# A fused convolution and two feed-forward layers: an accumulator's copy ahead of a rounding, three tiles in other places

## The chip, the core and the metric

The kernel runs on one core of one Trainium2 chip. Its engines are named as the profile names them: PE (TensorE, with PEld for its weight loads), DVE (VectorE), ACT (ScalarE), POOL (GpSimd) and SP, which here issues the DMAs and passes on notes between matmuls. The metric is the device time of one launch in microseconds (us), as the median of several runs. Lower is better.

## What is computed

```python
# x: (2, 4096, 192), weight_gen: (2, 4096, 8, 7), all float32
w = softmax(weight_gen, axis=-1)                   # 7 taps for each of 8 heads
out = sum over k of w[..., k] * x_padded[s + k]    # causal, 24 channels a head
x = out.reshape(8192, 192)
h = x @ w_in                                       # 192 -> 2048
x = where(h > 0, h, exp(min(h, 0)) - 1) @ w_out    # 2048 -> 192
h = x @ w_in2
return (h * clip(h + 3, 0, 6) / 6) @ w_out2        # 8192 x 192
```

## The kernel before

**Tiles and cells.** The 8192 tokens are cut into NB = 16 blocks of 512. Each of the two layers is worked block by block, and in a block the 2048 hidden columns are worked in NQ = 8 steps of 256. One such step is a cell (m, i, q): layer, block, step. There are 256 cells in one sequence, and the loop over n issues the work of cell n and of those around it. What orders the engines is the order in which this loop writes the instructions, for each engine is a queue worked from its head.

**One cell.** `matmuls` writes on PE the first product of cell n (into a pair of PSUM banks, `hset[n % 2]`) interleaved with the second product of cell n - 3 (LAG = 3), which adds into two accumulators: `acca` (two banks, used by alternate blocks) and `accb` (one bank, used by all blocks). Operands are split into a rounded high part and a low part, so a product is made of three. The two halves of the rows of PE are worked at once. After that, for k = 1 and then k = 0, `act_a` (ACT, L459 and L460 in the first layer, L462 in the second) and `gate` (DVE, L476 or L479) make the activation from bank k. `round_g` (ACT, L466) rounds the activations of cell n - 1 to `gh`, and `rest_g` (DVE, L470) makes the low part `gl`. In cells from n = 8 on, these two stand between k = 1 and k = 0, in cells before that behind k = 0.

**End of a block.** Three cells after the last cell of a block, `fold_b` (ACT, L332) copies `accb` to SBUF; one cell later `fold_a` copies `acca` and joins the two. As all blocks share `accb`, the first second-product matmul of the next block waits for the copy at L332.

**Weights.** The weights come as 64-bit floats and are turned into a high and a low part on the chip. A unit is 384 columns of this, of kind "i" (for `w_in`, to `wi`) or "o" (for `w_out`, to `wo`). Its steps: `begin` (ACT, L141: magnitude of the high word, to a work bank in PSUM, `aux` for "i" and `acca[1]` for "o"), s0, s1, s2 (DVE, L145, L148, L152: the float `f`), s3 (DVE, L157: a mask of the exponent, to the SBUF tile `tr`; and ACT, L159: the high part), s4 (DVE, L165: the rest `rr` from the low word `raw` and the mask). In the first layer PE then adds these up in the unit's bank (p5, L170 to L172) and ACT writes the low part out (p6, L177). In the second layer DVE does so (s5 and s6, L181 and L187). From group 4 on, the work bank of the first layer is the SBUF tile `f` itself, and the PSUM bank is used for the sum alone. `tr` and `rr` have two buffers each.

**Order of the weight work.** First-layer units form groups 0 to 8 (one unit, then pairs, then one unit). Groups 0 and 1 are written out ahead of the loop, groups 2 and 3 in cell 0; p5 and p6 of group n + 1 are written in cell n. So p5 of group 2 stands behind all of group 3 that uses the same banks. Second-layer units are steps of a `Stream`: each has a cell at which it begins and one at which it is due (`wtasks`), and the stream spreads its steps over the cells between.

**The convolution.** `attention` does the softmax on DVE and ACT and the products for a block on POOL (for block 0, on POOL and DVE). Block 1 has its products while the first weights are made. `prepare` transposes a block's result on PE into PSUM (L307, L310), ACT makes `xh` (L317), DVE makes `xl` (L319). Blocks 0 and 1 go through `hset[0]`, all later ones through `(acca[i % 2], aux)`. Block 1 is prepared in cell 5, behind p5 of group 6.

Of the kernel before, what the change touches and what calls it, by code (L numbers as in the profile page):

```python
# [9 lines left out]
F32R = mybir.dt.float32r  # L10
U32 = mybir.dt.uint32
# [6 lines left out]
def kernel(  # L18
# [21 lines left out]
    B, S, D = x.shape  # L40
# [4 lines left out]
    P = 128  # L45
# [3 lines left out]
    NF = DFF // P  # L49
    NQ = NF // 2  # L50
    HALO = K - 1
    LAG = 3
    TM = 4
    NB = TP // TM
# [26 lines left out]
    WI = [{k: cpool.tile([P, NQ * UN], F32R, name=f"wi{m}_{k}") for k in "hl"} for m in range(2)]  # L81

    WO = {0: cpool.tile([P, NF, 2 * D], F32R, name="wo0")}
    w_in = [w.bitcast(U32) for w in (w_in1, w_in2)]
    w_out = [w.bitcast(U32) for w in (w_out1, w_out2)]

# [23 lines left out]
    class Unit:  # L110
# [42 lines left out]
                self.f, self.hw, 0xC0000000, self.b, op0=ALU.bitwise_and, op1=ALU.bitwise_or)  # L153

        def s3(self):
            self.r = stage.tile([P, UN], U32, tag="tr", name="tr", bufs=2)
            nc.vector.tensor_scalar(self.r, self.f, 0xFF800000, None, op0=ALU.bitwise_and)  # L157
            hi, _, v = self.parts()
            nc.scalar.copy(hi, v(self.f.bitcast(F32)))  # L159

        def s4(self):
            f = o = self.r.bitcast(F32)
            if self.m == 0:
                o = self.rr = stage.tile([P, UN], F32R, tag="rr", name="rr", bufs=2)
            nc.vector.scalar_tensor_tensor(o, self.lw, 2.0**-52, f, op0=ALU.mult, op1=ALU.mult)  # L165

        def p5(self):
# [130 lines left out]
    def prepare(m, i):  # L298
        X = xts[m, i] = {
            k: act.tile([P, 2, XN], F32R, tag=f"x{k}", name=f"x{k}") for k in "hl"}  # L300
        v = lambda t: t[:, 0].rearrange("p (h c) -> p h c", h=2)
        if m == 0:

            (y, yd), ps = ya.pop(i), hset[0] if i < 2 else (acca[i % 2], aux)
            for t in range(TM):
                for h, p in enumerate(half):
                    nc.tensor.transpose(ps[h][:, t * HP:(t + 1) * HP], y[p, t, 0:P], ident[p, p])  # L307
            for s in range(2):
                for h, p in enumerate(half):
                    nc.tensor.transpose(ps[h][:, HN + s * HP:HN + (s + 1) * HP], yd[p, s], ident[p, p])  # L310
            parts = [(ps[h][:, 0:XN // 2], (lambda h: lambda t: v(t)[:, h])(h)) for h in range(2)]
        else:
            parts = [(zin.pop(i)[:, 0:XN], lambda t: t[:, 0])]

        def split():
            for src, w in parts:
                nc.scalar.copy(w(X["h"]), src)  # L317
            for src, w in parts:
                nc.vector.tensor_tensor(w(X["l"]), src, w(X["h"]).bitcast(F32), op=ALU.subtract)  # L319
            for k in "hl":  # L320
                for a in range(2):
                    later(1 if (m, i) == (0, 1) else 2, X[k][half[1 - a], 1].bitcast(F32), X[k][half[a], 0].bitcast(F32))
        return split
# [213 lines left out]
    for n in range(2 * NQ):  # L537
        c = NQ * (n + 2) if n < NB - 2 else start2 + (NQ if n % 2 else 0)
        groups.append([("io"[n % 2], 1, n // 2)])
        wtasks.append([c - 3, c + (3 if n < NB - 2 else 2 if n % 2 else 6), 1])  # L540
    made, fts = {}, {}

    def want(n):
# [28 lines left out]
    with tc.manual_schedule():  # L572
# [22 lines left out]
        for n in range(len(cells) + LAG + 3):  # L595
# [14 lines left out]
            for k in (1, 0):  # L610
# [3 lines left out]
                if not k and n < NQ:  # L614
                    for u in made[n + 1]:
                        u.p6()
                if k == (n >= NQ) and 1 <= n <= len(cells):
                    round_g(n - 1)
                    rest_g(n - 1)
                if not k:  # L620
                    continue
                for b in order:
                    if n == last[b] + LAG:
                        fold_b(*b)
                for b in order:
                    if n == last[b] + LAG + 1:
                        fold_a(*b)
# [49 lines left out]
```

## Time and profile before

| What | us |
|---|---|
| Median of 3 runs | 1254.43 (1254.25 to 1255.15) |
| The profiled execution, its own time | 1254.88 |
| Its span, first to last instruction | 1253.1 |
| PE busy (matmuls) | 1200.7 (96%) |
| DVE busy | 938.6 (75%) |
| ACT busy | 852.9 (68%) |
| POOL busy | 414.4 (33%) |

Busy is the time in which at least one instruction of the engine ran. PE is never far from full after the first tenth of the span, so a row that names PE as the one that waits is the first thing to look for. The number in square brackets at the end of a row of the timeline is the idle time ahead of it, with what ended it. Two matmuls run at once on the halves of PE's rows, and the recorded end of one is modelled; how much PE lost at a place is read better from the distance between the starts of matmuls than from the bracket. PEclk is the granted clock of PE as a share of 2.4 GHz; 0.50 is 1.2 GHz.

### The profile page before, as it was taken

To read this page: it belongs to the slowest core of one execution; us is meant where nothing else is said; L and a number is where in the kernel's file an instruction comes from. 1 tells how busy PE (TensorE), PEld (TensorE's weight loads), DVE (VectorE), ACT (ScalarE), POOL (GpSimd) and SP (SyncE) were. 2 spreads that over 40 slices of the span, in tenths; PEclk is the share of its full clock that TensorE was granted. 3 is DMA by queue.
4 is the path that set the end of the run, shared out by engine and by line. 5 is a ranking of instruction groups with operands and counts; after the bars stand their busy time and mean duration, and the time that the engine had idled before them with its cause. 6 is when DMAs were issued, how large, how long until landed. Compare 5 with 4: busy or idle time off the path is not lost.

```text
span 1253.1 us, 25450 instructions
## 1 busy us (share of the span) xinstructions
PE 1200.7 (96%) x10176; PEld 1093.3 (87%) x10176; DVE 938.6 (75%) x1224; ACT 852.9 (68%) x1340; POOL 414.4 (33%) x234
## 2 busy tenths in 40 slices
PE   3779999999999999999999999999999999999998
PEld 2457888888898888888888889999999999899996
DVE  7887989888988988898767666666666666666663
ACT  2557877887887887887886565566656655666563
POOL 7435886666787666688000000000000000000000
PEclk9789999999999999999999999999999999999999
DMA  6420222212222211221111111111111111110110
GB/s 158 125 97 27 87 86 87 71 44 60 87 87 87 83 59 35 84 87 51 50 53 44 34 52 51 39 52 52 28 38 52 51 51 39 52 51 25 41 39 26
DMA packets 33686, 75.82 MB, mean 61 GB/s; under 512 B 4644, under 2 KB 17058, under 8 KB 33568
## 3 DMA queue, kind: packets, MB, share of 16 engines
q1 hardware_dynamic: 33568, 74.19, 20.3%
q8 instruction: 80, 1.31, 0.5%
q14 instruction: 38, 0.31, 0.1%
HBM read 36.43 MB, written 12.58 MB: 39 GB/s over the span
## 4 chain that ended last, share of the span: by engine, by line
PE 68%; ACT 15%; DVE 12%; issue 3%; DMA 1%; SPq 0%; DVEq 0%; ACTq 0%
PE h L439 31%; PE acca L439 21%; PE accb L439 14%; DVE gl L470 5%; ACT gh L466 4%; ACT r L459 4%; ACT r L460 4%; DVE r L476 2%; DMA xl<-xl 1%; DVE tr L157 1%; DVE wt L230 1%; DVE aux L148 1%; DMA xt<-in_x_dram 1%; ACT fold L332 1%; ACT aux L141 0%
## 5 line engine op out<-in xcount | busy, mean ns | idle before, releaser
L439 PE MATMUL h<-xh,wi_l 64*128 64x512 f32 x1536 | 566.4, 397 | 1.6 <-ACT wi_l L177 1.6
L439 PE MATMUL h<-xh,wi_h 64*128 64x512 f32 x1536 | 559.0, 397 | 7.6 <-DVE xl L319 7.6
L439 PE MATMUL acca<-gh,wo 64*128 64x512 f32 x2048 | 561.3, 393 | 0.3
L439 PE MATMUL h<-xl,wi_h 64*128 64x512 f32 x1536 | 556.6, 396 | 0.8 <-DMA xl<-xl 0.8
L470 DVE TENSOR_TENSOR gl<-r,gh 128x1024 fp32r<-128x1024 f32 x256 | 377.3, 1474 | 56.7 <-ACT gh L466 55.3
L439 PEld LDWEIGHTS acca<-gh,wo 64*128 64x128 f32 x2048 | 378.4, 185 | 18.5 <-SPq L443 2.4
L439 PE MATMUL accb<-gh,wo 64*128 64x512 f32 x1024 | 326.0, 398 | 9.5 <-ACT fold L332 6.9
L462 ACT ACTIVATE r<-h,three 128x512 f32<-128x512 f32 x256 | 176.2, 688 | 227.3 <-PE h L439 221.7
L439 PE MATMUL accb<-gl,wo 64*128 64x512 f32 x1024 | 321.6, 393 | 0.0
L439 PE MATMUL acca<-gl,wo 64*128 64x512 f32 x1024 | 320.0, 392 | 0.0
L479 DVE SCALAR_TENSOR_TENSOR r<-r,h 128x512 f32<-128x512 f32 x256 | 176.0, 688 | 171.3 <-ACT r L462 170.5
L439 PEld LDWEIGHTS h<-xh,wi_h 64*128 64x128 f32 x1536 | 278.4, 186 | 21.2 <-DVE xl L319 8.1
L439 PEld LDWEIGHTS h<-xh,wi_l 64*128 64x128 f32 x1536 | 279.0, 186 | 15.3 <-ACT wi_l L177 2.9
L439 PEld LDWEIGHTS h<-xl,wi_h 64*128 64x128 f32 x1536 | 278.6, 186 | 13.7 <-DMA xl<-xl 1.5
L466 ACT CAST gh<-r 128x1024 fp32r<-128x1024 f32 x256 | 265.8, 1038 | 1.4 <-DVE r L479 0.8
L476 DVE SCALAR_TENSOR_TENSOR r<-r,h 128x512 f32<-128x512 f32 x256 | 174.1, 682 | 52.0 <-ACT r L460 51.5
L439 PEld LDWEIGHTS accb<-gh,wo 64*128 64x128 f32 x1024 | 185.9, 186 | 24.9 <-ACT fold L332 14.2
L439 PEld LDWEIGHTS acca<-gl,wo 64*128 64x128 f32 x1024 | 189.1, 185 | 8.0
L439 PEld LDWEIGHTS accb<-gl,wo 64*128 64x128 f32 x1024 | 189.3, 185 | 7.9
L265 POOL TENSOR_TENSOR tmp<-xt,wt 128x768 f32<-128x768 f32 (+1 forms) x96 | 193.5, 2016 | 7.0 <-DMA xt<-in_x_dram 0.8
L459 ACT ACTIVATE r<-h 128x512 f32<-128x512 f32 x256 | 152.7, 596 | 61.9 <-PE acca L439 31.3
L460 ACT ACTIVATE r<-r 128x512 f32<-128x512 f32 x256 | 162.0, 633 | 8.1
(102 smaller groups left out, 747.1 us busy)
## 6 DMA issues: line engine op xcount, KB each, us to landing
xt<-in_x_dram SPq DMA_DIRECT2D x14, 960.0 KB, 5.5
xh<-xh SPq DMA_DIRECT2D x64, 192.0 KB, 2.7
xl<-xl SPq DMA_DIRECT2D x64, 192.0 KB, 2.9
raw<-in_moe_w_out_dram SPq DMA_DIRECT2D x16, 384.0 KB, 3.2
z<-z SPq DMA_DIRECT2D x16, 384.0 KB, 2.3
zin<-z SPq DMA_DIRECT2D x16, 384.0 KB, 3.1
out_dram<-ot SPq DMA_DIRECT2D x16, 384.0 KB, 2.3
raw<-in_moe_w_in_dram SPq DMA_DIRECT2D x16, 192.0 KB, 3.3
```

The source lines that it names most:

```text
L148: nc.vector.tensor_scalar(self.b, self.b, 3, 0x3FFFFFF8, op0=ALU.logical_shift_left, op1=ALU.bitwise_and)
L157: nc.vector.tensor_scalar(self.r, self.f, 0xFF800000, None, op0=ALU.bitwise_and)
L230: v.tensor_tensor(w3, w3, mx.to_broadcast(shp), op=ALU.subtract)
L265: eng.tensor_tensor(o.rearrange("p t (h g) -> p t h g", g=G), xk, wk.rearrange("p (t h) g -> p t h g", h=H), op=ALU.mult)
L439: mm = nc.tensor.matmul(o, w, r, start=st, stop=sp).ins
L459: nc.scalar.activation(r, h, AF.Relu, scale=-1.0)
L460: nc.scalar.activation(r, r, AF.Exp, scale=-1.0)
L462: nc.scalar.activation(r, h, AF.Relu, bias=three)
L466: nc.scalar.copy(gg[n][0], rs[n])
L470: nc.vector.tensor_tensor(gl, rs.pop(n), gh.bitcast(F32), op=ALU.subtract)
L476: nc.vector.scalar_tensor_tensor(r, r, -1.0, h, op0=ALU.add, op1=ALU.max)
L479: nc.vector.scalar_tensor_tensor(r, r, 6.0, h, op0=ALU.min, op1=ALU.mult)
```

## The change

Five edits:

- `fold_b` is written ahead of `round_g` and `rest_g` in the cell in which both stand.
- The mask of s3 goes into the unit's PSUM work bank (`self.b`) instead of `tr`, for units of groups 0 to 3.
- `rr` of the first layer goes into `boot`, a tile with eight places that takes the room of the second layer's `wo1` before that is used, instead of two buffers of its own.
- Block 1 is transposed into `acca[1]` and `aux`, as later blocks are, instead of `hset[0]`.
- In `wtasks` of the last two second-layer units, the "i" unit is due three cells earlier (cell 131 instead of 134), the "o" unit begins and is due two cells earlier (131 to 136 instead of 133 to 138).

```diff
+    boot = cpool.tile([P, NF * 2 * D], F32R, tag="wo1", name="boot")
...
         def s3(self):
-            self.r = stage.tile([P, UN], U32, tag="tr", name="tr", bufs=2)
+            if self.m == 0 and self.n < 4:
+                self.r = self.b
+            else:
+                self.r = stage.tile([P, UN], U32, tag="tr", name="tr", bufs=2)
             nc.vector.tensor_scalar(self.r, self.f, 0xFF800000, None, op0=ALU.bitwise_and)
...
             if self.m == 0:
-                o = self.rr = stage.tile([P, UN], F32R, tag="rr", name="rr", bufs=2)
+                c = (2 * self.n + self.u) % NQ * UN
+                o = self.rr = boot[:, c:c + UN]
             nc.vector.scalar_tensor_tensor(o, self.lw, 2.0**-52, f, op0=ALU.mult, op1=ALU.mult)
...
-            (y, yd), ps = ya.pop(i), hset[0] if i < 2 else (acca[i % 2], aux)
+            (y, yd), ps = ya.pop(i), hset[0] if i == 0 else (acca[i % 2], aux)
...
-        wtasks.append([c - 3, c + (3 if n < NB - 2 else 2 if n % 2 else 6), 1])
+        wtasks.append([c - 3 - 2 * (n == NB - 1), c + (3 if n < NB - 1 else 0), 1])
...
+                if k:
+                    for b in order:
+                        if n == last[b] + LAG:
+                            fold_b(*b)
                 if k == (n >= NQ) and 1 <= n <= len(cells):
                     round_g(n - 1)
                     rest_g(n - 1)
                 if not k:
                     continue
-                for b in order:
-                    if n == last[b] + LAG:
-                        fold_b(*b)
```

How the instructions stand at three places follows. Lines further down than 83 have other numbers in the changed kernel: L141 is L143 there, L152 is L154, L157 is L162, L165 is L171, L187 is L193, L317 is L323, L319 is L325, L332 is L338, L459 and L460 are L465 and L466, L466 is L472, L470 is L476, L479 is L485.

ACT in the cell of the first block end, before; `fold` is the copy of `accb`, `gh` the rounding, and the numbers behind `h` tell the four banks apart:

```order
L459 ACTIVATE r<-h_73 128x512
L460 ACTIVATE r<-r 128x512
L466 CAST gh<-r 128x1024
L332 COPY fold<-accb 128x512
L459 ACTIVATE r<-h_72 128x512
L460 ACTIVATE r<-r 128x512
```

and in the changed kernel:

```order
L465 ACTIVATE r<-h_73 128x512
L466 ACTIVATE r<-r 128x512
L338 COPY fold<-accb 128x512
L472 CAST gh<-r 128x1024
L465 ACTIVATE r<-h_72 128x512
L466 ACTIVATE r<-r 128x512
```

The copy has changed places with the rounding of the cell before; nothing else moved there, and the same holds at the later block ends.

DVE from the second step of group 2 to the first of group 3, with the semaphores that each waits for, before:

```order
L152 SCALAR_TENSOR_TENSOR f<-raw,aux 128x384 [waits DMAHW6_49,DMAHW5_49,DMAHW7_49,DMAHW0_49,DVE_49]
L152 SCALAR_TENSOR_TENSOR f<-raw,acca_77 128x384 [waits DMAHW1_49,DVE_49]
L157 TENSOR_SCALAR tr<-f 128x384 [waits DVE_49] x2
L165 SCALAR_TENSOR_TENSOR rr<-raw,tr 128x384 [waits DVE_49]
L165 SCALAR_TENSOR_TENSOR rr<-raw,tr 128x384 [waits DVE_49,PE_49]
L145 TENSOR_SCALAR aux<-aux 128x384 [waits Activation_49]
```

and in the changed kernel:

```order
L154 SCALAR_TENSOR_TENSOR f<-raw,aux 128x384 [waits DMAHW6_49,DMAHW5_49,DMAHW7_49,DMAHW0_49,DVE_49]
L154 SCALAR_TENSOR_TENSOR f<-raw,acca_77 128x384 [waits DMAHW1_49,DVE_49]
L162 TENSOR_SCALAR aux<-f 128x384 [waits DVE_49]
L162 TENSOR_SCALAR acca_77<-f 128x384 [waits DVE_49]
L171 SCALAR_TENSOR_TENSOR boot<-raw,aux 128x384 [waits DVE_49]
L171 SCALAR_TENSOR_TENSOR boot<-raw,acca_77 128x384 [waits DVE_49]
L147 TENSOR_SCALAR aux<-aux 128x384 [waits Activation_49]
```

The order is the same; the masks lie in the two work banks, and the wait of s4 for PE is gone. In return ACT's L143 of group 3, which writes those banks, waits for DVE in the changed kernel, where L141 before waited for its DMAs alone.

DVE from the `xl` of second-layer block 1 on (cell 132), before; `wi_l` and `wo` are the low parts of the last two units:

```order
L319 TENSOR_TENSOR xl<-zin,xh 128x768
L187 TENSOR_TENSOR wi_l<-aux,tr 128x384
L479 SCALAR_TENSOR_TENSOR r<-r,h_75 128x512
L470 TENSOR_TENSOR gl<-r,gh 128x1024
L479 SCALAR_TENSOR_TENSOR r<-r,h_74 128x512
L145 TENSOR_SCALAR aux<-aux 128x384
```

and in the changed kernel:

```order
L325 TENSOR_TENSOR xl<-zin,xh 128x768
L150 TENSOR_SCALAR aux<-aux 128x384
L154 SCALAR_TENSOR_TENSOR aux<-raw,aux 128x384
L485 SCALAR_TENSOR_TENSOR r<-r,h_75 128x512
L476 TENSOR_TENSOR gl<-r,gh 128x1024
L485 SCALAR_TENSOR_TENSOR r<-r,h_74 128x512
L162 TENSOR_SCALAR tr<-aux 128x384
```

In cell 132 the last "i" unit was being finished, and is now done; the last "o" unit is at its second and third step, where it had not begun. Its low part is written in cell 135, before in cell 137; its first use is in cell 138.

## Rows read from the trace of the kernel before

**Rows 1.** Waits: engine, line, who is waited for: us, times, longest.

```profile
PE aux L170 <- DVE f L152: 21.4, 2, 12.8
...
PEld accb L439 <- ACT fold L332: 14.2, 17, 1.0
...
PE h L439 <- DVE xl L319: 7.6, 2, 5.0
...
PE accb L439 <- ACT fold L332: 6.9, 12, 0.6
...
PE accb L439 <- issue: 2.1, 1, 2.1
```

**Rows 2.** Timeline, ACT at a block's end: start us, us, instruction [idle].

```profile
153.48 1.03 ACT L466 CAST gh<-r 128x1024 fp32r<-128x1024 f32 x1
154.41 0.58 ACT L332 COPY fold<-accb 128x512 f32<-128x512 f32 x1
```

**Rows 3.** Timeline, PE at the same block's end.

```profile
152.21 0.40 PE L439 MATMUL accb<-gl,wo 64*128 64x512 f32 x1
...
153.85 0.40 PE L439 MATMUL acca<-gl,wo 64*128 64x512 f32 x1
...
154.09 0.40 PE L439 MATMUL acca<-gl,wo 64*128 64x512 f32 x1
155.04 0.50 PE L439 MATMUL accb<-gh,wo 64*128 64x512 f32 x1 [0.56 <-ACT fold L332]
...
155.39 0.39 PE L439 MATMUL accb<-gh,wo 64*128 64x512 f32 x1
```

**Rows 4.** Timeline, PE and DVE around PE's stop in the second layer.

```profile
703.60 0.39 PE L439 MATMUL h<-xh,wi_l 64*128 64x512 f32 x1
...
705.35 0.61 DVE L187 TENSOR_TENSOR wo<-aux,tr 128x256 fp32r<-128x256 f32 x2
...
706.07 0.47 PE L439 MATMUL accb<-gh,wo 64*128 64x512 f32 x1 [2.08 <-issue]
```

**Rows 5.** Timeline, DVE in groups 0, 2 and 3, and POOL's last product of block 1.

```profile
12.99 0.79 DVE L157 TENSOR_SCALAR tr<-f 128x384 uint32<-128x384 uint32 x1
...
36.04 0.57 DVE L145 TENSOR_SCALAR aux<-aux 128x384 f32<-128x384 f32 x1 [1.15 <-ACT aux L141]
...
38.83 1.97 DVE L157 TENSOR_SCALAR tr<-f 128x384 uint32<-128x384 uint32 x2
40.72 3.97 DVE L165 SCALAR_TENSOR_TENSOR rr<-raw,tr 128x384 fp32r<-128x384 uint32 x2
...
45.77 0.72 POOL L286 TENSOR_TENSOR y<-y,tmp 128x256 f32<-128x256 f32 x1
...
47.40 0.61 DVE L157 TENSOR_SCALAR tr<-f 128x384 uint32<-128x384 uint32 x2
```

**Rows 6.** Timeline, PE at the end of its first long stop.

```profile
47.07 1.65 PE L170 MATMUL aux<-f,ident 128*128 128x384 f32 x2 [8.63 <-DVE f L152]
```

**Rows 7.** Timeline, PE and ACT around the preparation of block 1.

```profile
83.24 0.47 PE L307 MATMUL h<-ident,y 64*128 64x64 f32 x8
...
84.90 0.54 ACT L177 CAST wo<-acca 128x256 fp32r<-128x256 f32 x2
...
89.11 0.79 PE L439 MATMUL h<-xh,wi_h 64*128 64x512 f32 x1 [5.00 <-DVE xl L319]
...
97.12 0.48 ACT L177 CAST wi_l<-aux 128x384 fp32r<-128x384 f32 x1 [0.16 <-PE aux L172]
...
98.58 0.40 PE L439 MATMUL h<-xh,wi_l 64*128 64x512 f32 x1
```

**Rows 8.** Windows: us, busy of PE, PEld, DVE, ACT, POOL, then PEclk, DMA.

```profile
84.12:86.87 2.75, 0.00 (x0) 0.00 (x0) 1.52 (x3) 2.75 (x7) 2.75 (x2) 1.00 0.17 46
89.11:93.69 4.58, 4.58 (x22) 3.64 (x24) 4.51 (x3) 0.00 (x0) 4.34 (x4) 0.50 0.00 0
703.99:706.07 2.08, 0.00 (x1) 0.04 (x2) 1.41 (x4) 0.69 (x1) 0.00 (x0) 1.00 0.00 0
```

## The prediction

> **What bounds the kernel now.** I read the table of waits first. PE is busy for 96% of the span, so nearly every microsecond PE waits is one that the kernel lasts longer, and what other engines wait for costs nothing by itself. The waits of PE have four large entries [rows 1]: the sum of the first weights waits for DVE's `f` (21.4 us in two waits, of which 12.8 is the start of the program, which the change does not touch, and 8.6 a stop in the start-up), the first product waits for DVE's `xl` (two waits, the longest 5.0), `accb` waits for ACT's copy (12 waits, 6.9), and one wait of 2.1 us has no releaser ("issue"). Then I read the timeline at each of the four. The five edits answer to these four places, and they are far apart in time, so I cost each alone and add.
>
> **The end of a block (first edit).** PE issues a pair of matmuls every 0.24 us (153.85 to 154.09). At the block end the next one comes at 155.04, and the one after it 0.35 later [rows 3]. So the stop costs 0.95 - 0.24 = 0.71, and the slow second pair another 0.11: 0.82, more than the bracket's 0.56. The last matmul into `accb` was over at 152.61 [rows 3], but ACT took the rounding first (153.48) and the copy after it (154.41 to 154.99) [rows 2]. In the changed order the copy starts where the rounding did, 153.48, as its data have been there for 0.87 us, and ends at 154.06. The matmul was due at 154.33, its weights some tenths before, so the stop goes but for a few hundredths. Twelve of them give 12 x 0.82 = 9.8 us. PEld has five more waits for the copy [rows 1]: with about 0.95 for each of the twelve, 14.2 - 11.4 = 2.8 us remain for the five, which PE feels at most in part, as four of them leave no idle time of PE in the table; I take 0.8. **Gain 10.6**, bounds 5 (half of it comes back because ACT runs later than here) and 12.6.
> The rounding and `rest_g` behind it start 0.58 us later (the copy's length). Behind them on ACT stand the activations of k = 0, whose start does not move, since the two ahead of them have only changed places; on DVE the gate of k = 0 stands behind `rest_g`. PE needs this `gh` two cells on. A cell lasts 1253/256 = 4.9 us, so a delay of 0.58 is covered many times over; without that cover it would cost 0.58 at each of 31 block ends, 18 us.
>
> **The last weights (fifth edit).** PE stands from 703.60 to 706.07, and goes on just behind the end of DVE's last `wo` piece (705.35 + 0.61 = 705.96) [rows 4]: the wait called "issue" is one for these weights. The changed table writes that piece two cells, about 9 us, earlier. The step distance less one pair is 2.47 - 0.24 = 2.2, with a slow pair 0.1 more. **Gain 2.3**, bounds 0 and 2.4. The added DVE and ACT steps in the cells before are the same steps, moved to cells where PE does not stand; DVE is busy for 75%.
>
> **The first weights (second and third edit).** The stop is 8.63 us, ended at 47.07 [rows 6]. PE waits there to use the two banks, and DVE must be through the steps of group 3 that use them. Group 2 starts on DVE at 36.04; its first six operations end at 38.83, so one every 0.465, each 0.57 long [rows 5]. These read or write PSUM. The masks then take 1.97 and s4 3.97 for two each, while POOL works on block 1; with POOL done (45.77 + 0.72) two masks of group 3 take 0.61 [rows 5]. What has all its operands in SBUF is held up while POOL runs; what has one in PSUM is not. In the changed kernel s3 and s4 each have one in PSUM, so I take 0.465 apart.
> Now the path in the changed kernel. ACT's next magnitude waits for s4 of the first unit, the new wait: nine operations from 36.04 on end at 36.04 + 8 x 0.465 + 0.57 = 40.33. ACT's operation (taken as long as DVE's on the same 384 columns, 0.57, with 0.1 for the hand-overs) gives 41.0. PE's banks are now free only after s4 of group 3, again nine operations: 41.0 + 3.72 + 0.57 = 45.3. The first unit's mask and s4 save 0.2 each (0.79 against 0.57 [rows 5]), and the whole start with them, 0.4. So PE goes on at 44.9 instead of 47.07. From there to the preparation of block 1 the cells hang on one another through ACT's L177 and the next unit's `f`, so I let the whole stretch move by that. The eight places of `boot` take two waits of DVE for PE away, but DVE waits for ACT's rounding behind them, so I give nothing for that. **Gain 2.2**, bounds -2.8 (below) and 4.
>
> A rule of the Trainium skill speaks against the masks' move: page "VectorE: DVE Perf Modes", section "The perf-mode tier table", gives fp32 `tensor_scalar` two results a cycle with both sides in SBUF, and one when any operand is in PSUM. The trace agrees where POOL is still (0.61 for two, [rows 5]). By that rule alone, an estimate from that page's clock of 0.96 GHz, each of the five masks on this path would be 0.2 us longer, and the sum 1 us smaller instead of larger. The 1.97 and 3.97 for two show that here the other rule weighs more, of page "SBUF — State Buffer", section "Who interferes with whom": DVE in a two-port mode, or with two SBUF inputs, shares ports with GpSimd.
>
> **Block 1 (fourth edit).** PE transposes at 83.24, then waits to 89.11 for DVE to have read `hset[0]` [rows 7]. The granted clock is full for the first 2.75 us of the stop and half from its end to 93.69 [rows 8], which costs another 4.58/2 = 2.3. In the changed kernel the transposes need `acca[1]` and `aux`, which ACT's L177 of group 6 reads until 84.90 + 0.54 = 85.44, a new wait of PE of 2.2 us. With 0.5 for the transposes, PE takes up matmuls at 86.0 instead of 89.11, and a stop of 2.08 us elsewhere did not lower the clock [rows 8], so it should stay up. At full clock the way from there to the low-part matmul of cell 7 (98.58 [rows 7]) is (98.58 - 89.11) - 2.3 = 7.2, so PE would be there at 93.2. But that matmul needs ACT's L177 of 97.12, and this one stands on ACT behind the next unit's high part, made from an `f` that DVE makes while POOL works; nothing of that is freed by the change, and POOL, which waits for these transposes, starts 2.2 us later. If L177 stays at 97.12 + 0.48, PE goes on at 97.65: a gain of 0.9 with a new stop of some 4.4 us. This is near the stop of 5.0, after which the clock was low for 4.58 us of work; that would take 2.3 back. Between +0.9 and -1.4 I take **-0.3**; the upper bound is 98.58 - 93.2 = 5.4, if L177 comes earlier with everything else.
>
> **Sum.** 10.6 + 2.3 + 2.2 - 0.3 = 14.8 us. The profiled execution took 1254.88 (span 1253.1 and 1.8 around it): 1240.1 after the change. The median of the runs shown is 0.45 lower, so I predict 1239.6.
>
> **Rivals.** (1) *The hold-up does not go with PSUM.* If s3 and s4 in PSUM form still take 1.97 and 3.97 beside POOL, group 2 ends at 44.7 as before, ACT's new wait adds 0.7, and group 3 needs 2.8 for six operations and 1.7 for masks and s4 without POOL: 49.9, so 2.8 lost instead of 2.2 gained: 1244.6. Against: the operations with one PSUM operand in the same seconds take 0.57.
> (2) *Block 1 is not held by ACT's L177.* PE then gains 5.4 instead of -0.3: 1233.9. For it: POOL starts later and may leave DVE free for longer.
> (3) *The copy comes no earlier where it counts.* If it then waits for PE's last `accb` matmul, 10.6 is lost: 1250.2. Against: that matmul was over 0.87 us before ACT came.
> (4) *The change does not do what it says for the last weights*: they are written earlier but come late all the same, as their data are not loaded. 1241.9.
> (5) *Slower than before.* The rounding, now behind the copy, comes too late for the second product: 0.58 at each of 31 block ends is 18.0 us, 1257.6. It decides once `gh` and `gl` have less than 0.58 us to spare before PE wants them; the spare is more than one cell, 4.9 us, so this is remote.
>
> **How the numbers follow.** Forecast 1239.6: 0.68. Rival 1: 0.10; rival 2: 0.09; rival 3: 0.06; rival 4: 0.05; rival 5: 0.02. The forecast's own terms spread by about 4 us to each side (block ends 9.5 to 12, start-up 0.5 to 4, block 1 -1.4 to 2). With rivals 1, 2 and 4 largely in, the range is 1234.5 to 1246.0. About 0.2% (2.5 us) is what a measurement of this kernel can tell from no change, so "the same" is 1251.9 to 1256.9. Rivals 1 to 4 all end faster than that alone; only two of the losses together reach it. So faster 0.93, the same 0.04, slower 0.03.
>
> **What would show it.** In the profile after: no row "PE accb <- ACT fold", the copy at a block end starting under 0.1 us behind the activation of k = 1, and block ends 0.8 us closer together; no stop of PE near 690 to 706 and the "issue" row gone; masks and s4 of groups 1 to 3 at about 0.56 each, and the first long stop of PE ending near 45 instead of 47.07; the row "PE h <- DVE xl" with 5.0 us gone, in its place a wait of the transposes of about 2.2 us for ACT's L177, and a new stop in cell 7 for `wi_l`. Wrong would be: masks over 1 us each while POOL runs (rival 1), no stop in cell 7 (rival 2), PE still waiting at block ends (rival 3).

## The result and the profile after

The changed kernel took 1238.95 us (median of 4 runs, 1236.53 to 1241.36), the kernel before beside it 1254.79 (1254.25 to 1255.64). The ratio is 0.9873, with a 95% interval from 0.9846 to 0.9900: about 16 us faster. The prediction was 1239.6, range 1234.5 to 1246.0. The four times lie in two groups, 1236.53 and 1236.65, and 1241.24 and 1241.36; the profiled execution is the one of 1236.65 (span 1234.9), 18.2 us of span shorter than the profiled one of before. All medians here are of fast executions; one execution of e2_copy_layer1 was slow, with 3017.05 us, and is left out.

I cut the span at marks that both traces have (the restart of PE for the sum of group 2, and the first `accb` matmul behind the copy at a block end) and compare stretch by stretch:

| Stretch | before, us | after, us | difference | forecast |
|---|---|---|---|---|
| start to the sum of group 2 | 47.07 | 42.25 | -4.8 | -2.2 (first weights) |
| to the first block end | 70.84 | 68.34 | -2.5 | +0.3 (block 1) |
| next 15 block ends | 554.79 | 543.70 | -11.1 | -10.6 (block ends) |
| the block with the last weights | 37.86 | 35.62 | -2.2 | -2.3 (last weights) |
| the rest, to the end | 542.5 | 545.0 | +2.4 | 0 |
| sum | 1253.1 | 1234.9 | -18.2 | -14.8 |

Two terms came as forecast, the start gained 5.4 us more, and one loss of 2.4 us was not in the forecast at all. The second profile of the changed kernel (below) gained 12.4 in place of 18.2, all of the difference in the start.

The waits of the changed kernel, beside [rows 1] (waiting engine and line, who is waited for: us, times, longest):

```profile
PE aux L176 <- DVE boot L171: 7.1, 1, 7.1
PE h L445 <- ACT wi_l L183: 5.4, 4, 2.5
ACT fold L338 <- PE accb L445: 3.0, 16, 0.2
PE h L445 <- DVE xl L325: 2.6, 1, 2.6
PE acca L313 <- ACT wo L183: 2.3, 1, 2.3
```

PE's waits for `fold` and the "issue" entry are gone. At block ends the wait has turned round: ACT's copy now waits for PE's last `accb` matmul, 16 times, never over 0.2 us. The 2.3 us of the transposes is new. The 5.4 for `wi_l` are four stops (before: three, 1.6 in all), and only 0.98 of them lies in cell 7, where the prediction had a new one. The longest, 2.49 at 55.32, stands between the sums of groups 3 and 4; with the copy's edit alone there is one of 2.37 at the same place.

Timeline of ACT at the first block end, beside [rows 2] (start us, us, instruction):

```profile
145.51 0.63 ACT L466 ACTIVATE r<-r 128x512 f32<-128x512 f32 x1
146.05 0.57 ACT L338 COPY fold<-accb 128x512 f32<-128x512 f32 x1
146.51 1.05 ACT L472 CAST gh<-r 128x1024 fp32r<-128x1024 f32 x1
```

and of PE there, beside [rows 3]:

```profile
146.39 0.40 PE L445 MATMUL h<-xl,wi_h 64*128 64x512 f32 x1
...
146.62 0.41 PE L445 MATMUL h<-xh,wi_l 64*128 64x512 f32 x1
...
146.88 0.40 PE L445 MATMUL accb<-gh,wo 64*128 64x512 f32 x1
...
147.12 0.39 PE L445 MATMUL accb<-gh,wo 64*128 64x512 f32 x1
```

The copy ends at 146.62, the next `accb` matmul starts at 146.88, and the steps around it (0.23, 0.26, 0.24) are those of any other pair.

Windows of the changed kernel over the 15 block ends and over the block with the last weights (us, busy of PE, PEld, DVE, ACT, POOL, then PEclk, DMA), beside [rows 4]:

```profile
110.59:654.29 543.70, 542.92 (x4730) 496.34 (x4728) 480.86 (x605) 450.04 (x727) 350.59 (x182) 1.00 0.24 70
...
654.29:689.91 35.62, 35.62 (x307) 33.68 (x304) 26.22 (x37) 21.91 (x31) 0.00 (x0) 1.00 0.16 46
```

and the same two stretches before:

```profile
117.91:672.70 554.79, 546.95 (x4732) 482.41 (x4730) 480.86 (x602) 450.00 (x727) 350.69 (x182) 1.00 0.23 69
672.70:710.56 37.86, 35.78 (x304) 31.85 (x306) 27.54 (x39) 21.79 (x31) 0.00 (x0) 1.00 0.15 43
```

After the change PE is busy for all but 0.8 us of the first stretch and for the whole second one: no stop is left. Before, it was idle for 7.8 and 2.1 us in them.

Timeline of DVE in groups 2 and 3, beside [rows 5]:

```profile
33.10 0.57 DVE L147 TENSOR_SCALAR aux<-aux 128x384 f32<-128x384 f32 x1 [1.22 <-ACT aux L143]
...
35.89 0.55 DVE L162 TENSOR_SCALAR aux<-f 128x384 uint32<-128x384 uint32 x1
...
36.81 0.55 DVE L171 SCALAR_TENSOR_TENSOR boot<-raw,aux 128x384 fp32r<-128x384 uint32 x1
...
37.94 0.57 DVE L147 TENSOR_SCALAR aux<-aux 128x384 f32<-128x384 f32 x1
```

Mask and rest take 0.55 each, where two of them took 1.97 and 3.97; POOL works beside them here too, from 35.76 to 37.57 in one instruction. PE beside [rows 6 and 7], at the sum of group 2, the transposes of block 1 and the low parts of cell 7:

```profile
42.25 1.01 PE L176 MATMUL aux<-f,ident 128*128 128x384 f32 x1 [7.09 <-DVE boot L171]
...
80.62 0.25 PE L313 MATMUL acca<-ident,y 64*128 64x64 f32 x1 [2.28 <-ACT wo L183]
...
91.30 0.50 PE L445 MATMUL h<-xh,wi_l 64*128 64x512 f32 x1 [0.98 <-ACT wi_l L183]
```

The stop of 5.00 us for `xl` is now two, of 2.28 and 0.98. The windows at half clock in this trace, beside [rows 8]:

```profile
39.97:46.80 6.83, 4.55 (x9) 2.90 (x10) 3.98 (x8) 4.00 (x9) 4.61 (x4) 0.50 0.73 225
80.93:84.34 3.41, 3.41 (x25) 3.13 (x23) 2.85 (x5) 1.71 (x4) 2.87 (x2) 0.50 0.00 0
```

The granted clock (0.50, that is 1.2 GHz) fell behind the stop of 2.28 us, which ended at 80.62, although the prediction had it stay up.

### The profile page after: what moved, and what is told of

Read it like the earlier page. It is cut to its first block, busy times and chain, and to the rows that moved or that the text cites. A ratio compares the mean times of both kernels' runs of the same rounds, so it can differ in the third digit from the quotient of the medians.

```text
span 1234.9 us, 25476 instructions
## 1 busy us (share of the span) xinstructions
PE 1192.9 (97%) x10176; PEld 1090.2 (88%) x10176; DVE 927.6 (75%) x1224; ACT 854.3 (69%) x1340; POOL 415.5 (34%) x234
## 4 chain that ended last, share of the span: by engine, by line
PE 93%; DVE 2%; ACT 2%; DMA 1%; issue 1%; POOL 1%; SPq 0%; DVEq 0%; ACTq 0%; POOLq 0%
PE h L445 43%; PE acca L445 29%; PE accb L445 19%; DMA raw<-in_moe_w_in_dram 1%; DVE f L154 1%; ACT r L465 0%; PE acca L313 0%; ACT r L466 0%; PE aux L369 0%; DMA raw<-in_moe_w_out_dram 0%; ACT gh L472 0%; ACT wo L164 0%; DVE h L271 0%; DMA xl<-xl 0%; SPq L507 0%
## 5 line engine op out<-in xcount | busy, mean ns | idle before, releaser
L445 PE MATMUL h<-xh,wi_l 64*128 64x512 f32 x1536 | 578.7, 396 | 5.4 <-ACT wi_l L183 5.4
L445 PE MATMUL h<-xh,wi_h 64*128 64x512 f32 x1536 | 574.7, 395 | 2.6 <-DVE xl L325 2.6
L445 PE MATMUL h<-xl,wi_h 64*128 64x512 f32 x1536 | 572.0, 394 | 0.8 <-DMA xl<-xl 0.8
L476 DVE TENSOR_TENSOR gl<-r,gh 128x1024 fp32r<-128x1024 f32 x256 | 377.4, 1474 | 71.7 <-ACT gh L472 69.2
L445 PEld LDWEIGHTS h<-xh,wi_l 64*128 64x128 f32 x1536 | 284.8, 186 | 19.8 <-ACT wi_l L183 7.2
L445 PEld LDWEIGHTS h<-xh,wi_h 64*128 64x128 f32 x1536 | 285.1, 186 | 15.9 <-DVE xl L325 2.8
L485 DVE SCALAR_TENSOR_TENSOR r<-r,h 128x512 f32<-128x512 f32 x256 | 175.8, 687 | 161.2 <-ACT r L468 160.3
L445 PEld LDWEIGHTS h<-xl,wi_h 64*128 64x128 f32 x1536 | 284.5, 186 | 14.0 <-DMA xl<-xl 1.5
L472 ACT CAST gh<-r 128x1024 fp32r<-128x1024 f32 x256 | 266.4, 1040 | 2.3 <-DVE r L482 1.5
L465 ACT ACTIVATE r<-h 128x512 f32<-128x512 f32 x256 | 152.5, 596 | 49.6 <-PE acca L445 31.7
L466 ACT ACTIVATE r<-r 128x512 f32<-128x512 f32 x256 | 162.1, 633 | 8.1
```

What stands on the lines that cost most here:

```text
L445: mm = nc.tensor.matmul(o, w, r, start=st, stop=sp).ins
L465: nc.scalar.activation(r, h, AF.Relu, scale=-1.0)
L466: nc.scalar.activation(r, r, AF.Exp, scale=-1.0)
L472: nc.scalar.copy(gg[n][0], rs[n])
L476: nc.vector.tensor_tensor(gl, rs.pop(n), gh.bitcast(F32), op=ALU.subtract)
L485: nc.vector.scalar_tensor_tensor(r, r, 6.0, h, op0=ALU.min, op1=ALU.mult)
```

## The experiments

"Less" and "more" are against the kernel before in the same session, where nothing else is said. With start-ups that differ by up to 6 us from one profile of a kernel to the next, I read the stretches of each trace beside the medians.

**The changed kernel again (e0_after_again).** No edit.

> The changed kernel once more. Its four times fell into two groups, 1236.5 and 1241.3 us. Theory C: the groups differ in the start-up, in when the granted clock falls to 0.50 and rises again there. A run of the slower group then shows the start of block 2 later by some 4 to 5 us against the profiled run of 1236.65, and the same distance from there to the end. Rival D: the 4.7 us are spread over the blocks (some 0.15 us at each of 31), and the start-up is the same. If the profile falls into the quicker group again, its marks agree with the first one's within 0.5 us and nothing is told apart.

Median 1240.85 (1238.45 to 1242.51), ratio 0.9887 [0.9873, 0.9902]. The profile caught a run of 1242.51. Against the first profile its marks lie 0.1 us later at the sum of group 1, 2.1 at group 2, 0.8 at group 7, 5.8 at the first block end, and 5.9 at the end. So theory C stands: nearly all of it lies in the start, and the clock goes with it. It rose at 34.84 here and at 29.73 in the first profile, and the way from the sum of group 1 to that of group 2 was 14.41 against 12.46. The largest step is in cell 7, on PE:

```profile
94.95 0.79 PE L445 MATMUL h<-xh,wi_l 64*128 64x512 f32 x1 [3.80 <-ACT wi_l L183]
```

and in the window that begins in this stop:

```profile
92.87:99.70 6.83, 4.75 (x22) 3.77 (x24) 5.25 (x5) 3.38 (x7) 6.52 (x5) 0.50 0.00 0
```

This is what the prediction described: a new stop for `wi_l` (forecast 4.4, here 3.80), after which the clock takes back what was won. Part of why the first profile had only 0.98 is seen on DVE and POOL. There DVE's `gl` started just ahead of POOL:

```profile
81.45 1.22 DVE L476 TENSOR_TENSOR gl<-r,gh 128x1024 fp32r<-128x1024 f32 x1 [1.07 <-ACT gh L472]
```

```profile
81.47 2.61 POOL L271 TENSOR_TENSOR y<-xt,wt 128x768 f32<-128x768 f32 x1 [36.73 <-PE aux L316]
```

and in this run POOL was first:

```profile
83.83 2.52 DVE L476 TENSOR_TENSOR gl<-r,gh 128x1024 fp32r<-128x1024 f32 x1 [1.07 <-ACT gh L472]
```

```profile
83.72 1.55 POOL L271 TENSOR_TENSOR y<-xt,wt 128x768 f32<-128x768 f32 x1 [38.88 <-PE aux L316]
```

Whoever starts first takes its short time, and the other one is held for about 1 us more. That DVE delay goes on through the next unit's `f` to ACT's high part and `wi_l` behind it: it starts 10.17 us behind the transposes in the first profile (90.79 - 80.62) and 11.45 here (94.44 - 82.99).

This 1.3 is less than half of the 2.8 between the two stops. The other 1.5 is PE itself, which came to cell 7 later in the first profile, having worked 3.4 us at half clock behind the transposes. The profile of e2_copy_layer1 (below) has both at once: the clock fell at the transposes (0.50 from 82.64 to 86.05), POOL was first (83.03 against 83.08 for `gl`), and the stop lies between:

```profile
94.28 0.49 PE L444 MATMUL h<-xh,wi_l 64*128 64x512 f32 x1 [2.32 <-ACT wi_l L182]
```

The order of the two follows the clock as well. In the eight other profiles of kernels with the fourth edit `gl` starts 0.83 to 0.84 us behind the transposes' start; POOL, which waits for the transposes, starts 0.72 to 0.73 behind it in the four where the clock stayed up there and 0.85 to 1.04 in the four where it fell.

**The copy alone (e1_copy).** The kernel before with `fold_b` ahead of `round_g`:

```diff
+                if k:
+                    for b in order:
+                        if n == last[b] + LAG:
+                            fold_b(*b)
                 if k == (n >= NQ) and 1 <= n <= len(cells):
```

> The kernel before with the first edit alone: the copy of accb ahead of the rounding at every block end. The prediction's step gives 10.6 us less, so 1244.2. The trace after the whole change shows 11.1 us won in the 15 block ends of the first layer and 2.3 us lost in the second layer, whose blocks last 36.02 us in place of 35.85. Theory S: that loss belongs to this edit (with no late copy the two half-row streams of matmuls run abreast, and abreast they take about 1% longer); then 8.8 less, 1246.0, and blocks of 36.0 in the second layer. Rival R: the loss belongs to another edit; then 11.1 less, 1243.7, and blocks of 35.85. The stop of 2.1 us at the last weights is there by both.

Median 1245.28 against 1254.74, ratio 0.9921 [0.9906, 0.9936]. In the trace the 15 block ends take 543.80 us in place of 554.79: 11.0 won. The second layer's blocks last 35.86:

```profile
806.14 0.40 PE L439 MATMUL accb<-gh,wo 64*128 64x512 f32 x1
...
842.00 0.39 PE L439 MATMUL accb<-gh,wo 64*128 64x512 f32 x1
```

That is rival R: the loss in the second layer does not come with the copy. The median is 9.5 less, the profiled run (1242.93) 12 less; the three longer executions of this kernel were not profiled. Their mean granted clock was 0.988 against 0.991 in the profiled one, so they had more time at half clock; where, stays open.

**The copy ahead in the first layer alone (e2_copy_layer1).** The changed kernel with

```diff
-                        if n == last[b] + LAG:
+                        if n == last[b] + LAG and not b[0]:
                             fold_b(*b)
```

and the old place for the second layer.

> The whole change, but with the copy ahead of the rounding only at the block ends of the first layer; in the second layer it stands behind the rounding as before. Theory S: the late copy sets the two half-row streams apart again, the second layer's blocks last 35.85 us as before, and the kernel takes 2.3 us less than the changed one, 1234.3 against 1236.6 in the quicker group. Rival R: the blocks stay at 36.0 and the waits for the copy come on top, 0.1 to 0.3 us at each of 15 block ends: 1.5 to 4.5 us more than the changed kernel.

Median 1240.34 (three executions) against 1240.85 for the changed kernel in the same session. The blocks of the second layer last 36.02 as with the whole change, so theory S fell here too; the price that rival R put on the late copy there fell with it. In the second layer the order of copy and rounding makes no difference: from the seventeenth block end to the last both traces take 504.26 us.

**The first weights alone (e3_first_weights).** The kernel before with the masks of groups 0 to 3 in PSUM and the rests in `boot`:

```diff
+            if self.m == 0 and self.n < 4:
+                self.r = self.b
...
+                o = self.rr = boot[:, c:c + UN]
```

> The kernel before with the second and third edit alone: masks of groups 0 to 3 in PSUM, the rests in eight places of their own. The prediction's step gives 2.2 us less, 1252.6. The trace after the whole change shows the sum of group 2 earlier by 4.8 us, of which 1.0 lies in the first 24 us, 1.9 in a clock that was at 1.00 already at 29.7 (before: 35.7), and 1.9 in the steps of groups 2 and 3. If the clock's part belongs to these edits, 4.8 to 5.0 less, 1250; if it was a chance of that run, 2.9 less, 1251.9.

Median 1254.81 against 1254.74, ratio 1.0000 [0.9991, 1.0009]: nothing, where 1250 or 1251.9 was expected. But in the trace the sum of group 2 starts earlier:

```profile
44.63 1.01 PE L175 MATMUL aux<-f,ident 128*128 128x384 f32 x1 [6.61 <-DVE boot L170]
```

That is 2.4 us less (2.2 forecast), 3.1 at the first block end, and the same 3.1 at the sixteenth. Then 1.7 is lost in the block with the last weights, most of it behind the stop, where the clock fell:

```profile
704.47:707.88 3.41, 3.41 (x19) 2.97 (x18) 1.58 (x2) 2.21 (x3) 0.00 (x0) 0.50 0.36 115
```

and 2.4 more by blocks of 36.02 us (817.19 to 853.21) in the second layer. So the loss in the second layer comes with edits 2 and 3. In this trace the clock rose at 35.45, near the 35.68 of the kernel before, and not at 29.73 as in the first profile after.

All profiles together part the two. From the sum of group 1 to that of group 2 the kernels without the masks' move take 16.26 to 16.28 us where the clock rises between 34.36 and 35.79, and 16.54 in the one where it rises at 29.52 (e6_room, next). With the move it is 14.41 to 14.42 in the four that rise between 34.84 and 35.45, 13.61 in the one at 31.78, and 12.45 to 12.48 in the four between 29.05 and 29.98. So the masks' move alone wins 1.85 on this way, and an early clock 1.95 more with the move, and nothing in the one profile without it.

**The rests' room alone (e6_room).** The third edit alone, with `wo1` in its old place.

> The kernel before with the third edit alone: the rests of the first layer in eight places of boot, the masks still in tr; three is placed so that wo1 keeps its place at byte 91,840. The prediction put the whole gain of the first weights on the masks' move and nothing on the room: masks of group 2 near 2 us for two and rests near 4 for two while POOL works, the sum of group 2 at 46.5 to 47, about 1254.7. Rival (the waits of DVE for PE that go with the room are what counts): the sum of group 2 at 43.9 to 44.6, as in the kernel with both edits, 2 to 3 us less up to there.

Median 1255.10 against 1255.42, ratio 0.9998 [0.9988, 1.0007]. DVE in group 2:

```profile
37.45 2.72 DVE L159 TENSOR_SCALAR tr<-f 128x384 uint32<-128x384 uint32 x2
40.10 3.97 DVE L168 SCALAR_TENSOR_TENSOR boot<-raw,tr 128x384 fp32r<-128x384 uint32 x2
```

The sum of group 2 starts at 46.45 (9.73 of stop), though the clock rose early here and DVE began these masks 1.4 us sooner than before. With the masks in `tr`, both steps are held beside POOL as before, and the room alone wins nothing: the gain is the masks' move, as forecast. The masks' move with two buffers for `rr` wasn't tried: s4 would then wait for the sum of the group before, and that sum for the s4 of this group, which shares its banks. So by the order of the program the room is needed, though it wins nothing; no run shows that part.

**Block 1 alone (e4_block1).**

```diff
-            (y, yd), ps = ya.pop(i), hset[0] if i < 2 else (acca[i % 2], aux)
+            (y, yd), ps = ya.pop(i), hset[0] if i == 0 else (acca[i % 2], aux)
```

> The kernel before with the fourth edit alone: block 1 transposed into acca[1] and aux. The prediction's step gives 0.3 us more (1255.0): 0.9 won, and 2.3 lost again where the granted clock falls at a new stop in cell 7. The two profiles of the changed kernel differ here: 2.4 us won between the sum of group 6 and the end of the first block in the one, 1.1 lost in the other, where the clock was at 0.50 for 6.8 us from 92.9 on. So either about 1252.4 or about 1255.8, by whether the clock falls again in cell 7; the second layer as before (35.85 us a block).

Median 1255.79 against 1255.91, ratio 0.9999 [0.9989, 1.0009]. In the trace PE is 5.4 us ahead at the sum of group 7, then stops in cell 7 for 3.80 us:

```profile
97.34 0.79 PE L439 MATMUL h<-xh,wi_l 64*128 64x512 f32 x1 [3.80 <-ACT wi_l L177]
```

and works behind it at half clock:

```profile
97.23:100.64 3.41, 3.30 (x16) 2.62 (x18) 3.31 (x4) 1.44 (x4) 3.25 (x3) 0.50 0.00 0
```

The transposes waited 2.29 for L177, as the step said, and the clock stayed up there. From the sum of group 6 to the first block end it loses 0.6. So the path of the step came as described; the medians, with an interval from 1.4 less to 1.1 more, cannot tell 0.3 more from nothing.

But this is one of two ways that the start goes. In the nine profiles of kernels with this edit the transposes stop for 2.28 to 2.32 us. In five the clock falls there (the first one of the changed kernel, and e2, e8, e10 and e11, some of them below), and the stop in cell 7 is 0.98 to 2.32, or gone in e10. In four it stays up there (e0, e4, e9, e12), and cell 7 has a stop of 3.80 to 3.83, in or behind which the clock falls. From the sum of group 6 to the first block end the first way takes 34.5 to 35.9 (38.4 in e10, which has a stop of its own), the second 37.2 to 37.9; it was 36.9 before. All four profiles in which the clock first rose before 30 us went the first way, and one of the other five; what decides between them was not found.

**The last weights alone (e7_last).**

```diff
-        wtasks.append([c - 3, c + (3 if n < NB - 2 else 2 if n % 2 else 6), 1])
+        wtasks.append([c - 3 - 2 * (n == NB - 1), c + (3 if n < NB - 1 else 0), 1])
```

> The kernel before with the fifth edit alone: the last two weight units earlier. The prediction's step gives 2.3 us less, 1252.4, with the stop near 704 gone and everything else as before. Rival: the stop goes but its time comes back, since the extra steps of DVE and ACT now stand in cells 128 to 135; then a difference under 1 us.

Median 1252.52 against 1255.91, ratio 0.9973 [0.9963, 0.9982]: 3.4 less, with the interval 2.3 to 4.6. The block with the last weights:

```profile
672.15:707.53 35.38, 35.38 (x306) 29.63 (x304) 26.24 (x37) 21.83 (x31) 0.00 (x0) 1.00 0.16 46
```

That is 2.5 us shorter than before (37.86), and nothing comes back. In the profiles where the clock falls behind this stop (first weights alone, block 1 alone), its block takes 1.7 and 1.6 more; this may be the rest of the 3.4, but is only argued.

**The place of the weights (e8_wo1_moved, e9_all_moved).** What edits 2 and 3 change in the second layer is room alone. `boot` claims the room of `wo1` earlier, so `wo1` starts at byte 91,808 of each partition and no longer at 91,840, and the activations lie 3,072 bytes lower, as two `rr` buffers are gone. In the first kernel only `wo1` is moved back, in the second all five weight tiles go up by 32 bytes; the edit is one moved line each:

```diff
+    three = cpool.tile([P, 1], F32, name="three")
     boot = cpool.tile([P, NF * 2 * D], F32R, tag="wo1", name="boot")
...
-    three = cpool.tile([P, 1], F32, name="three")
```

(in the second kernel ahead of `WI`).

> The changed kernel with the small tile three placed ahead of boot. So wo1, the output weights of the second layer, start at byte 91,840 of each partition, as in the kernel before, and no longer at 91,808; nothing else moves. Theory P (the place of the weights): the second layer's blocks lasted 35.85 us in the two kernels with wo1 at 91,840 (before, the copy alone) and 36.02 in the four with 91,808, so the 32 bytes are the cause; then 35.85 again here, 15 to 16 times 0.17 = 2.6 us less than the changed kernel. Rival Q: the activations (x, g, r), which all lie 3,072 bytes lower in those four kernels and here too, are the cause; then 36.02 and no gain.

Median 1236.68 (1234.34 to 1239.20), ratio 0.9851 [0.9832, 0.9870]. A block of the second layer, first of the changed kernel, then of this one:

```profile
797.99 0.40 PE L445 MATMUL accb<-gh,wo 64*128 64x512 f32 x1
...
834.00 0.40 PE L445 MATMUL accb<-gh,wo 64*128 64x512 f32 x1
```

```profile
798.16 0.39 PE L446 MATMUL accb<-gh,wo 64*128 64x512 f32 x1
...
834.00 0.40 PE L446 MATMUL accb<-gh,wo 64*128 64x512 f32 x1
```

36.01 against 35.84, and the kernel before had 35.84 too:

```profile
818.11 0.39 PE L439 MATMUL accb<-gh,wo 64*128 64x512 f32 x1
...
853.95 0.40 PE L439 MATMUL accb<-gh,wo 64*128 64x512 f32 x1
```

Theory P holds, rival Q falls: the 2.4 us lost in the second layer are 32 bytes of `wo1`. e6_room says the same from the other side: its activations lie 3,072 bytes lower as well, its `wo1` at 91,840, and its blocks last 35.81 to 35.86.

> The changed kernel with the small tile three placed ahead of all weights instead: the five weight tiles all start 32 bytes higher, each at a multiple of 64 bytes, which in the kernel before only wo1 did; nothing else moves. Theory P with output weights alone: the second layer as in the kernel before, 2.6 us less, and the first layer's 15 blocks also 0.17 us shorter (36.31 to 36.14), together 5.1 us less than the changed kernel. If the input weights count too, whose matmuls are over half of all, more than that, some 8 to 11 us less. Rival Q: no difference.

Median 1235.73 (1232.67 to 1236.04), ratio 0.9838 [0.9823, 0.9853].

```profile
800.52 0.39 PE L446 MATMUL accb<-gh,wo 64*128 64x512 f32 x1
...
836.26 0.39 PE L446 MATMUL accb<-gh,wo 64*128 64x512 f32 x1
```

35.74: the input weights count too. From the first block end to the last it is 5.7 us quicker than the changed kernel; the 8 to 11 expected for this case did not come. In the first layer the first 12 blocks gain only 0.07 each, the later ones 0.15 to 0.29. Its profiled start was a bad one (5.2 us behind at the first block end), so the whole gain does not show in one run.

**The place of the activations (e11_act_moved, e12_both_off).** A 32-byte tile at the head of the `act` pool moves x, g, r and z by 32 bytes, once with the weights of e9_all_moved and once with those of the changed kernel:

```diff
+    act.tile([P, 8], F32, name="pad", bufs=1)
     hset = [[psp.tile([P, 512], F32, name=f"h{i}{k}") for k in range(2)] for i in range(2)]
```

> The changed kernel with all weights at multiples of 64 bytes, and with every tile of the act pool (x, g, r, z) 32 bytes higher, so that the moving operands of the matmuls no longer start at multiples of 64. Theory P1 (only the weights' place counts): blocks of 35.74 us in the second layer as with the weights moved alone, the same time within the spread of the start-up. Theory P2 (the moving operands' place counts as well, or only the distance between the two): blocks of 36.0 us or more, 3 us or more lost over 15 blocks.

Median 1240.87 (1236.70 to 1241.59), ratio 0.9886 [0.9870, 0.9903]:

```profile
797.98 0.40 PE L447 MATMUL accb<-gh,wo 64*128 64x512 f32 x1
...
834.00 0.39 PE L447 MATMUL accb<-gh,wo 64*128 64x512 f32 x1
```

36.02, and every block of both layers lasts within 0.04 us what it lasts in the changed kernel. The moving operands count as well (P2).

> The changed kernel with the tiles of the act pool (x, g, r, z) 32 bytes higher and the weights where it has them: now all weights and all moving operands start 32 bytes past a multiple of 64. So far a block of the second layer took 36.02 us with all weights 32 off and the activations on a multiple, 36.02 with the weights on a multiple and the activations 32 off, 35.85 with wo1 and the activations on one, 35.74 with all on one. Theory A (each operand has to start at a multiple of 64 bytes): 36.02 or more here. Theory B (only the distance between the weights and the moving operand counts, it has to be a multiple of 64): 35.74 here, and some 5 to 6 us less than the changed kernel between the first block and the last.

Median 1234.68 (1232.77 to 1236.54), ratio 0.9832 [0.9814, 0.9849]:

```profile
799.32 0.39 PE L446 MATMUL accb<-gh,wo 64*128 64x512 f32 x1
...
835.21 0.39 PE L446 MATMUL accb<-gh,wo 64*128 64x512 f32 x1
```

35.89 lies between the two expectations (36.02 or more, 35.74). So neither holds as it was put: in the second layer the distance between weights and moving operands counts, and something beside it. In the first layer the 15 block ends take 542.17, as in e9_all_moved (542.16; 543.71 in the changed kernel), so there theory B fits.

**Group 8 later (e10_last_group).** e9_all_moved with the last first-layer unit due one cell later, to take the stop of cell 7 away:

```diff
-    wtasks = [[0, n - 2, len(g)] for n, g in enumerate(groups)]
+    wtasks = [[0, n - 2 + (n == NQ), len(g)] for n, g in enumerate(groups)]
```

> The changed kernel with all weights at multiples of 64 bytes, and with group 8 of the first weights (the last wo unit) due one cell later: its last three DVE steps and ACT's high part stand behind the work of cell 6 in place of ahead of it. Theory: the stop of PE in cell 7 (0.98 to 3.83 us in the profiles so far) is ACT's low part of wi standing behind that high part, which waits 5.4 to 6.7 us for DVE's f beside POOL. Then the low part comes at about 90, the stop goes, and the granted clock stays at 1.00 there: up to 3.8 + 1.7 = 5.5 us less than the 1236.0 of the profile with the same addresses, 1231 in the median. Rival: the ring through ACT and DVE finds its next wait in cell 8 (the sum of group 8 or gh), and PE stops there for as long: 1235 to 1236.

Median 1236.25 (1234.71 to 1238.45), ratio 0.9849 [0.9834, 0.9864]; 1235.73 without the edit. ACT writes `wi_l` at 88.59, 7.7 us behind the transposes in place of 10.2 to 11.5, and the stop in cell 7 is gone, so its cause is shown. But the sum of group 8 now waits for its own rest:

```profile
98.12 0.69 PE L179 MATMUL acca<-boot,plus 128*128 128x384 f32 x1 [2.48 <-DVE boot L172]
```

and the clock is at 0.50 from 97.68 to 104.51. The rival was right: the ring through DVE and ACT finds its next wait.

## Why the prediction was right, and where not

- **Block ends: right.** 10.6 forecast, 11.1 in the trace after and 11.0 with this edit alone. Counting the distance between starts of pairs (0.82 a stop), and not the bracket (0.56), gave the size: the first twelve of these 15 blocks became 0.85 shorter each. The cover named for the later rounding held.
- **Last weights: right.** 2.3 forecast, 2.2 after, 2.5 with this edit alone. The difference is the slower place of `wo1` within the same block: with `wo1` moved back it takes 35.39 in the changed kernel too, against 35.62.
- **First weights: right mechanism and size, in part hidden by the clock.** Edits 2 and 3 alone win 2.4 against 2.2 forecast, and the experiment with the room alone puts it on the masks, as the step said. The 4.8 in the profile after has 1.95 more from a clock that rose early in that run; the prediction gave the clock no part here.
- **Block 1: right for one way of two, wrong in its ground for the clock.** The wait of 2.2 for L177 (2.28), the new stop of 4.4 (3.80) and the clock taking back the gain all came, with the edit alone and in one of two profiles of the whole change; 0.3 more was forecast; 0.6 more came with the edit alone and 1.1 more in that profile. In the other profile the stop was 0.98 and 2.4 were won. The step that failed is "a stop of 2.08 us elsewhere did not lower the clock [rows 8], so it should stay up": a stop of 2.07 to 2.08 at that same place was followed by a fall in two experiments, and the stop of the transposes in five of nine profiles. That the -0.3 lies between what the two ways give is luck.
- **What was missed.** The prediction gave nothing for where tiles lie. `boot` moved `wo1` by 32 bytes, which cost 2.4 us over the second layer. The forecast came out within 1 us of the median partly by luck: this loss and the better start of some runs lie against each other.
- **The rivals.** Rival 1 fell (0.55 for a mask at 35.89, beside POOL); rival 3 fell (the copy starts right behind the activation); rival 4 fell (no stop at the last weights); rival 5 fell (no wait for `gh` on PE). Rival 2 came in part in the first profile. Of the 2.8 us by which the stop in cell 7 was shorter there, 1.3 came by the way it named (DVE was freer because POOL came later, behind `gl`), and 1.5 by one that it did not name, PE coming later at half clock.

## What to carry to other kernels

Where one engine is full, put ahead on the others what frees its banks, and behind it what is wanted a cell later; read the gain from the distance of starts. A change of tiles also moves those allocated behind or in their place: compare the starting bytes of the matmul operands of both programs before reading a small difference. And a stop that is short can cost as much again in the clock behind it, in one run and not in the next, so a start-up is judged by several runs.

## What the runs showed of the hardware

**The place of matmul operands counts by 32 bytes.** Starting bytes modulo 64, and a block of the second layer:

| Kernel | wi1 | wo1 | x, g | block, us |
|---|---|---|---|---|
| before, e1, e4, e6, e7, e8 | 32 | 0 | 0 | 35.81 to 35.87 |
| after, e0, e2, e3 | 32 | 32 | 0 | 36.01 to 36.03 |
| e9_all_moved, e10 | 0 | 0 | 0 | 35.73 to 35.75 |
| e11_act_moved | 0 | 0 | 32 | 36.02 |
| e12_both_off | 32 | 32 | 32 | 35.89 |

The groups of PE's instructions in 400 us of the second layer show some of it in the mean of a matmul (the number ahead of the last bar, in ns), first of the changed kernel, then with all weights moved:

```profile
L445 PE MATMUL h<-xh,wi_h 64*128 64x512 f32 x534 | 199.0, 393 | 0.0
```

```profile
L446 PE MATMUL h<-xh,wi_h 64*128 64x512 f32 x537 | 199.2, 391 | 0.0
```

The ends of matmuls are modelled, and this group has 393 in the kernel before too, so the blocks, measured from start to start, are the better evidence. What in the chip makes this difference was not found. e9_all_moved and e12_both_off, which gain 5.7 and 3.5 us over the changed kernel from the first block end to the last, also have the lowest medians of all that ran: 1235.73 and 1234.68, against 1238.95 and 1240.85 for the changed kernel. Four runs each, with starts that vary, do not tell these two apart.

**The clock's fall behind a stop varies.** The stop of 2.04 to 2.08 us at the last weights left the clock at 1.00 in the kernel before, in it [rows 8] and in the 6.8 us behind it, and also with the copy alone and with the room alone; it was followed by 3.4 us at 0.50 with the first weights alone and with block 1 alone. The stop of 2.28 to 2.32 at the transposes was followed by a fall in five profiles and by none in four. The Trainium skill (page "TensorE: Matmul & The Clock Gate", section "Part 1: The HAM clock gate (the "warmup" mystery)") says that the watch on PE's activity runs freely and does not start anew with a kernel. The varying falls would agree with that, but no run here tests it.
